# Exponentials over pairs of adjacent PSUM banks in an attention loop that also computes row maxima

## The chip, the cores and the metric

The kernel runs on one NeuronCore of a Trainium2 chip. A core has five engines that run their own instruction queues and meet through semaphores: TensorE (PE in the profile; its weight loads stand in a row of their own, PEld), VectorE (DVE), ScalarE (ACT), GpSimd (POOL) and SyncE (SP), which here issues DMAs. Matmul results land in PSUM, which has 8 banks; a bank holds 128 partitions of 512 fp32 values. The metric is the device time of one execution in microseconds.

## The reference, cut to what matters

Two blocks work on the same `x` of 2048 tokens by 640 channels, and a gate mixes them.

```python
g = sigmoid((x * gate_w).sum(-1, keepdims=True))
# attention: 32 heads of 20 channels, 2048 tokens
q, k, v = split(x @ wqkv)
scores = einsum("bhqd,bhkd->bhqk", q, k) * 20 ** -0.5
a = einsum("bhqk,bhkd->bhqd", softmax(scores), v) @ wo
# token-mixing MLP: over the token axis, 1728 hidden units
b = (gelu(layernorm(x)^T @ w1 + b1) @ w2 + b2)^T
out = g * a + (1 - g) * b
```

The change touches only the attention: scores, their exponentials and the sums with `v`.

## The kernel before, in words

Values are split into a high and a low part, so that fp32r matmuls (one pass) give nearly fp32 results: a product needs three of them. In the attention the three parts are stacked in the contraction instead, three times 20 rows a head. Two heads form a pair `p`; head `j=0` of a pair stands on partitions 0 to 63 and `j=1` on 64 to 127 of `ks` and `qs`, the two row halves of PE. Matmuls on different halves run side by side.

The softmax needs a maximum for each query. It is found one pair ahead: `s_next` runs one step of a stream, a matmul with queries on the partitions and 512 keys along the row (tile `s`, 60 rows of contraction, L178) and a VectorE reduction over it (L180). The stream takes the two halves in turn, `j=1` first. When the 64 tiles of half the queries are done, `s_max` and `s_store` gather the maxima, negate and split them, and send them through memory to two more rows of `qs`. So the score matmul in the loop itself (tile `st`, 62 rows of contraction, L700) gives score minus maximum, with keys on the partitions and queries along the row.

Before the loop come the projections and the MLP, into whose matmuls the first 736 of 2048 maximum tiles are mixed (`S_AHEAD`). The loop over the 16 pairs has 32 iterations for each, 512 in all: two halves of the queries (`qh`) by 16 blocks of 128 keys (`kt`). One iteration makes

- four score tiles of 128 keys by 512 queries, for `j` in two halves and `c` in two column blocks of 512 queries, each followed by an exponential on ScalarE (L703) that writes `p` to SBUF (`pt`, 12 buffers);
- `take` maximum tiles. The 1312 left (`LEFT`) are spread so that an iteration has two or three of them, and the last ones none;
- four products of `p` with `v` (tile `pv`, L637) on four column groups of PE, for the exponentials of the iteration before (`pend`, `pv_flush`); fp32 operands make two matmul instructions of each, eight in all. After 16 iterations `pv_evac` copies `pv` out on VectorE (L618), and POOL issues DMAs.

PE, ScalarE, VectorE, POOL and SP run in the order in which the program is written (`manual_schedule`). On PE an iteration is: score, maximum, score, maximum, score, maximum if `take` is 3, score, pv. `turn` chooses the halves so that a score tile and the maximum tile next to it lie on different halves. A PSUM tile is given out in turn from its tag's buffers; the matmul that reuses a buffer waits for the engine that read it. Tags are `st` (four banks), `s` (three banks) and `pv` (one): all eight banks. If `take` is 2, the third score tile takes a bank of `s` ("lent", L709). The same `st` tag serves the projections and the MLP ahead of the loop and the output product behind it.

Of the kernel before, what the change touches and what calls it, by code (L numbers as in the profile page):

```python
# [7 lines left out]
F32 = mybir.dt.float32  # L8
# [5 lines left out]
P = 128  # L14
S, D, H, DH, F = 2048, 640, 32, 20, 1728
# [13 lines left out]
def gated_mix(ctx, tc, xT, x, wqk, wv0, wv1, wo, w1, w1t, b1, w2, b2, out):  # L29
    nc = tc.nc  # L30
    EG = mybir.EngineType
    ctx.enter_context(tc.manual_schedule(engines={EG.PE}))
    PSUM = bass.MemoryType.PSUM
# [30 lines left out]
    cp = ctx.enter_context(tc.tile_pool(name="cp", bufs=1))  # L64
    base = ctx.enter_context(tc.tile_pool(name="base", bufs=1))
    psum = ctx.enter_context(tc.tile_pool(name="psum", bufs=1, space=PSUM))

    def st_tile(shape, name):
        return psum.tile(shape, F32, tag="st", bufs=4, name=name)

    def s_tile(shape, name):
        return psum.tile(shape, F32, tag="s", bufs=3, name=name)
# [44 lines left out]
    def base_stack(p, full, eng=nc.sync):  # L117
        ks = k8([P, S], F32R, f"ks{p}_{full}")
        qs = [q4([P, S // 2], F32R, f"qs{p}_{full}_{i}") for i in range(2)]
        load_stack(p, ks, qs, full, eng)  # L120
        return ks, qs

    def load_m(p, qs, half, put=nc.sync.dma_start):
        src = m_d[p, half].rearrange("(g i j t) r -> i j t g r", i=2, j=2, t=8)
        for j in range(2):
            for i in range(2):
                r = 64 * j + 3 * DH + i
                dst = qs[half].bitcast(F32)[r: r + 1, :].rearrange("o (t g r) -> o t g r", g=4, r=32)
                put(dst, src[i: i + 1, j])
# [3 lines left out]
    def load_v(p):  # L133
        v_tiles[p] = base.tile([P, NT, NPAIR], F32, tag="v", bufs=2, name=f"v{p}")
        c0 = NPAIR * (p % 8)
        nc.sync.dma_start(v_tiles[p], v_d[p // 8, :, :, c0: c0 + NPAIR].rearrange("t p c -> p t c"))
# [18 lines left out]
    def s_next():  # L155
        next(stream)()
        for e in list(s_close):
            e[0] -= 1
            if e[0] <= 0:
                s_close.remove(e)  # L160
                e[1]()

    def s_finish():
        next(stream, None)
        while s_close:
            s_close.pop(0)[1]()
# [46 lines left out]
    def qk_unit(m, w, q):  # L213
        wh, wl = w
        ps = st_tile([P, 512], f"qk{m}_{q}")
        mm3(ps, [(wh[:, c], wl[:, c], xh[c][q], xl[c][q]) for c in range(NC)])
        hi = p1.tile([P, 512], F32R, tag="evh", bufs=2, name=f"evh{m}_{q}")
        lo = p1.tile([P, 512], F32R, tag="evl", bufs=2, name=f"evl{m}_{q}")
        hi_lo(hi, lo, ps, hi_eng=nc.scalar)
        dst = q_d if m < NC else k_d  # L220
        rows = slice((m % NC) * P, (m % NC + 1) * P)
        cols = slice(q * 512, (q + 1) * 512)
        nc.sync.dma_start(dst[0, rows, cols], hi.bitcast(F32))
        nc.sync.dma_start(dst[1, rows, cols], lo.bitcast(F32))
# [12 lines left out]
    warm = p1.tile([P, 512], F32R, tag="evh", bufs=2, name="warm")  # L237
    nc.vector.memset(warm.bitcast(F32), 0.0)
    wps = st_tile([P, 512], "warm_ps")
    for i in range(10):  # L240
        nc.tensor.matmul(wps, warm[:, :P], warm, start=(i == 0), stop=(i == 9))
# [51 lines left out]
    for half in range(2):  # L293
        wvh, wvl = wvs[half]
        width = HALF + 2 if half == 0 else HALF
        for t in range(NT):
            n = NT * half + t
            if n == NT - 2:
                for i in range(4):
                    stats_load(i)  # L300
            if n == NT:
                nc.vector.tensor_scalar_mul(negm, gs[:, :, 1], -1.0 / D)
            if n in (2, 4, 6, 8, 10):
                split_wv(1, n // 2 - 1)
            if n == 2 * NT - 4:
                w[2] = load_w(2)
            ps = st_tile([P, width], f"v{half}_{t}")
            q, cols = t // 4, slice((t % 4) * P, (t % 4 + 1) * P)
            mm3(ps, [(xh[c][q][:, cols], xl[c][q][:, cols], wvh[c], wvl[c]) for c in range(NC)])
            vt = pvp.tile([P, 16, VW], F32, tag="vt", bufs=3, name=f"vt{half}_{t}")  # L310
            nc.gpsimd.memset(vt[:, :, DH], 1.0)
            nc.scalar.activation(vt[:, :, :DH], ps[:, :HALF].rearrange("p (h w) -> p h w", w=DH), AF.Copy)
            nc.sync.dma_start(v_d[half, t], vt.rearrange("p h w -> p (h w)"))
            if half == 0:
                nc.vector.tensor_copy(gs[:, t], ps[:, HALF:])
            else:
                stats_unit(t)
                stats_load(t + 4)
# [253 lines left out]
    lp = lps.enter_context(tc.tile_pool(name="lp", bufs=1, side="right"))  # L572

    def s_stack(p):
        ks = lp.tile([P, S], F32R, tag="sk", bufs=2, name=f"sk{p}")
        qs = [lp.tile([P, S // 2], F32R, tag="sq", bufs=4, name=f"sq{p}_{i}") for i in range(2)]
        load_stack(p, ks, qs, False)
        return ks, qs
# [52 lines left out]
    def pv_flush():  # L631
        while pend:
            p, qh, kt, pv, pts = pend.pop(0)
            for j in range(2):
                for c in range(2):
                    r = 32 * (2 * j + c)
                    nc.tensor.matmul(pv[r: r + 32, :], v_tiles[p][:, kt, 10 * j: 10 * j + 32], pts[j, c],  # L637
                                     start=(kt == 0), stop=(kt == NT - 1))
            if kt == NT - 1:
                pv_evac(p, qh, pv)  # L640
# [4 lines left out]
    def load_wo(c):  # L645
        raw = ap.tile([P, D], F32, tag="wor", bufs=1, name=f"wor{c}")
        nc.gpsimd.dma_start(raw, wo[c * P:(c + 1) * P, :])
        hi_lo(woh[c], wol[c], raw, hi_eng=nc.gpsimd, lo_eng=nc.gpsimd)
# [15 lines left out]
    def o_early(q, hi_eng=nc.scalar, lo_eng=nc.vector):  # L664
        o_hl[q] = o_part(q, slice(0, (NC - 1) * P), NC - 1, 256, "e", 2, hi_eng, lo_eng)
# [1 line left out]
    def o_late(q):  # L667
        return o_part(q, slice((NC - 1) * P, D), 1, 512, "l", 4, nc.scalar, nc.vector)[0]

    turn = given = 0  # L670
    LEFT = NP * 128 - S_AHEAD
    for p in range(NP):
        ks, qs = st_src[p]
        if 8 <= p < 8 + NC:
            load_wo(p - 8)
        for it in range(32):
            qh, kt = divmod(it, NT)
            if p + 1 < NP:
                if it == 6:
                    st_src[p + 1] = base_stack(p + 1, True)  # L680
                if it == 12:
                    load_v(p + 1)
                if it == 27:
                    load_m(p + 1, st_src[p + 1][1], 0)
            if it == 11 and p:
                load_m(p, qs, 1)
            if it == 14 and due_stack:
                n = due_stack.pop()
                if n < NP:
                    s_src[n] = s_stack(n)  # L690
            if p == NP - 1 and it in (20, 26):
                o_early(it // 26, nc.gpsimd, nc.gpsimd)
            if kt == 0:
                pv = psum.tile([P, 512], F32, tag="pv", bufs=1, name=f"pv{p}_{qh}")
            pts = {}

            def st_op(j, c, tile):
                r = slice(64 * j, 64 * j + 3 * DH + 2)
                ps = tile([P, 512], f"st{p}_{it}_{j}{c}")
                nc.tensor.matmul(ps, ks[r, kt * P:(kt + 1) * P], qs[qh][r, c * 512:(c + 1) * 512],  # L700
                                 start=True, stop=True)
                pt = lp.tile([P, 512], F32, tag="pt", bufs=12, name=f"p{p}_{it}_{j}{c}")
                nc.scalar.activation(pt, ps, AF.Exp, scale=SCALE)  # L703
                pts[j, c] = pt

            due = min((p * 32 + it + 1) * LEFT // (NP * 32 - 28) + 1, LEFT)
            take = min(due - given, 3)
            for n in range(4):
                st_op((n + turn) % 2, n // 2, s_tile if n == 2 and take < 3 else st_tile)  # L709
                if n < take:  # L710
                    s_next()
            given += take
            if take and given == LEFT:
                s_finish()
            turn = (turn + take) % 2
            pv_flush()
            if p * 32 + it in later:
                later.pop(p * 32 + it)()
            pend.append((p, qh, kt, pv, pts))
    pv_flush()  # L720
    ordered.close()
    lps.close()

    ep = ctx.enter_context(tc.tile_pool(name="ep", bufs=1, side="right"))
    tys = [ep.tile([P, 2, HALF], F32, name=f"oy{t}") for t in range(NT)]
# [13 lines left out]
    for t in range(NT):  # L739
# [5 lines left out]
        ps = [st_tile([P, HALF], f"a{t}_{i}") for i in range(2)]  # L745
        a_mms(t, ps, o_hl[t // 2], slice((t % 2) * P, (t % 2 + 1) * P), range(NC - 1))
    for t in range(NT):
        ps = [st_tile([P, HALF], f"b{t}_{i}") for i in range(2)]
# [49 lines left out]
```

## Time and profile before

| | us |
|---|---|
| median of 3 runs (1844.1 to 1847.46) | 1844.79 |
| the profiled execution: its span | 1844.8 |
| PE busy | 1829.7 |
| DVE busy | 1428.9 |
| ACT busy | 1361.6 |
| first and last exponential of the loop start | 699.5 and 1761.7 |

The span runs from the first to the last instruction and is the device time itself; nothing lies around it. In the rows of the profile, a group is a source line, engine, operation and tile, with its count, its busy time (overlaps counted once), the mean duration of one in ns, and the idle time of the engine just ahead of its instructions with what ended it. A busy share is not the share of time that work needs: neighbouring instructions of an engine overlap, and an engine whose instruction waits in its pipeline counts as busy. Timeline rows give the start, the length, the engine, the operation, how many were merged into the row, and in brackets the idle time ahead of it. The recorded ends of matmuls are modelled.

### The profile page before, as it was taken

How to read it: one execution, taken by the hardware profiler on the slowest of the kernel's cores; microseconds unless marked ns; L12 is line 12 of the kernel's file. 1: busy time of each engine (PE TensorE's matmuls, PEld its weight loads, DVE VectorE, ACT ScalarE, POOL GpSimd, SP SyncE). 2: the span in 40 equal slices, each digit the busy share in tenths (PEclk: the TensorE clock that was granted, in tenths of full speed). 3: DMA queues.
4: the chain of work that ended last, by engine and by line, in shares of the span. 5: the costliest groups of instructions: out<-in, count | busy, mean ns of one | idle time of the engine just before them, and what ended most of it. 6: DMA issues, size and time to landing. Idle time of an engine off the chain costs nothing. (4 is left out here: it accounts for less than half of the span.)

```text
span 1844.8 us, 39129 instructions
## 1 busy us (share of the span) xinstructions
PE 1829.7 (99%) x14978; PEld 1135.2 (62%) x14978; DVE 1428.9 (77%) x2341; ACT 1361.6 (74%) x2688; POOL 637.1 (35%) x900
## 2 busy tenths in 40 slices
PE   9999999999999999999999999999999999999998
PEld 7998799999999994333333333333333333333378
DVE  4202299999999998888888888888888888888137
ACT  4243244465444448999999999999999999999930
POOL 1013478888887770112112111121321211212210
PEclk9999999999999999999999999999999999999999
DMA  8456766566645645504032324213540423301463
GB/s 289 143 169 212 222 173 173 158 194 193 168 139 166 189 136 121 118 15 103 20 85 61 73 42 93 57 50 78 107 103 24 109 47 77 71 14 23 131 219 132
DMA packets 152831, 216.61 MB, mean 117 GB/s; under 512 B 65698, under 2 KB 92082, under 8 KB 148738
## 3 DMA queue, kind: packets, MB, share of 16 engines
q1 hardware_dynamic: 129172, 178.68, 35.4%
q0 software_dynamic: 14688, 20.78, 5.2%
q10 hardware_dynamic: 8784, 14.65, 2.4%
q8 instruction: 118, 1.93, 0.4%
q14 instruction: 69, 0.57, 0.1%
HBM read 165.43 MB, written 48.25 MB: 116 GB/s over the span
## 5 line engine op out<-in xcount | busy, mean ns | idle before, releaser
L180 DVE TENSOR_REDUCE mx<-s 128x1 f32<-128x512 f32 x2048 | 1293.7, 684 | 159.9 <-PE s L178 119.7
L703 ACT ACTIVATE p<-st 128x512 f32<-128x512 f32 x2048 | 1042.1, 615 | 20.9 <-PE s L178 2.2
L700 PEld LDWEIGHTS st<-qs_True,ks_True 62*128 62x128 f32 x2048 | 307.3, 185 | 485.1 <-ACT p L703 312.9
L700 PE MATMUL st<-qs_True,ks_True 62*128 62x512 f32 x2048 | 579.6, 425 | 0.2 <-ACT ty L477 0.2
L637 PE MATMUL pv<-p,v 128*32 128x512 f32 x4096 | 555.5, 605 | 0.2
L178 PE MATMUL s<-sk,sq 60*128 60x512 f32 x1280 | 423.1, 434 | 0.0
L41 POOL TENSOR_TENSOR wl<-wr,wh 128x512 fp32r<-128x512 f32 x228 | 273.6, 1216 | 59.8 <-ACT wh L38 30.9
L624 POOL DMA_DIRECT2D o_d<-oev x128 | 67.0, 524 | 494.3 <-DVE oev L618 491.6
L178 PE MATMUL s<-ks_False,qs_False 60*128 60x512 f32 x768 | 225.1, 397 | 0.4 <-DVE mx L180 0.3
L46 PE MATMUL y<-gh,wh 64*128 64x320 f32 x896 | 216.8, 308 | 0.0
L46 PE MATMUL y<-gl,wh 64*128 64x320 f32 x832 | 210.3, 306 | 0.0
L46 PE MATMUL y<-gh,wl 64*128 64x320 f32 x832 | 209.4, 305 | 0.0
L38 ACT ACTIVATE wh<-wr 128x512 fp32r<-128x512 f32 (+2 forms) x246 | 135.9, 594 | 90.2 <-PE s L178 29.0
L178 PEld LDWEIGHTS s<-sk,sq 60*128 60x128 f32 x1280 | 197.7, 185 | 1.2
L637 PEld LDWEIGHTS pv<-p,v 128*32 128x32 f32 x4096 | 84.9, 108 | 171.4 <-issue 156.4
L46 PE MATMUL u<-hl,wh 64*128 64x320 f32 x864 | 167.1, 306 | 0.0
L46 PE MATMUL u<-hh,wh 64*128 64x320 f32 x864 | 167.1, 306 | 0.0
L46 PE MATMUL u<-hh,wl 64*128 64x320 f32 x800 | 156.9, 306 | 0.4 <-POOL wl L41 0.4
L46 PEld LDWEIGHTS y<-gh,wh 64*128 64x128 f32 x896 | 155.3, 184 | 0.4
L46 PEld LDWEIGHTS y<-gh,wl 64*128 64x128 f32 x832 | 147.0, 184 | 0.3
L46 PEld LDWEIGHTS y<-gl,wh 64*128 64x128 f32 x832 | 146.9, 184 | 0.0
L178 PEld LDWEIGHTS s<-ks_False,qs_False 60*128 60x128 f32 x768 | 124.4, 184 | 1.1 <-DVE mx L180 1.1
(124 smaller groups left out, 1817.6 us busy)
## 6 DMA issues: line engine op xcount, KB each, us to landing
wr<-in_w_dram SPq DMA_DIRECT2D x196, 256.0 KB
ks_True<-k_d SPq DMA_DIRECT2D x96, 160.0 KB
qs_True<-q_d SPq DMA_DIRECT2D x192, 80.0 KB
sk<-k_d SPq DMA_DIRECT2D x60, 160.0 KB
sq<-q_d SPq DMA_DIRECT2D x120, 80.0 KB
v_d<-vt SPq DMA_DIRECT2D x32, 168.0 KB
v<-v_d SPq DMA_DIRECT2D x16, 336.0 KB
xr<-in_xT_dram SPq DMA_DIRECT2D x20, 256.0 KB
```

What stands on the lines that cost most here:

```text
L38: nc.scalar.activation(hi, src, AF.Copy)
L41: (lo_eng or nc.vector).tensor_sub(lo, src, hi.bitcast(F32))
L46: nc.tensor.matmul(ps[k], a[r], b[r], start=start, stop=stop)
L178: nc.tensor.matmul(ps, qs[half][r, t * P:(t + 1) * P], ks[r, kc * 512:(kc + 1) * 512], start=True, stop=True)
L180: nc.vector.tensor_reduce(mx[:, kc, j, t: t + 1], ps, axis=AX.X, op=OP.max)
L624: nc.gpsimd.dma_start(o_d[DH * h: DH * h + DH, cols], ev[r: r + DH, :])
L637: nc.tensor.matmul(pv[r: r + 32, :], v_tiles[p][:, kt, 10 * j: 10 * j + 32], pts[j, c], start=(kt == 0), stop=(kt == NT - 1))
L700: nc.tensor.matmul(ps, ks[r, kt * P:(kt + 1) * P], qs[qh][r, c * 512:(c + 1) * 512], start=True, stop=True)
L703: nc.scalar.activation(pt, ps, AF.Exp, scale=SCALE)
```

## The change

The two score matmuls of one column block, one for each head, write the two halves of one tile of two adjacent banks, and one exponential reads both banks, 1024 columns, and writes a `pt` tile of twice the width (6 buffers, the same bytes). An iteration has two such pairs, `c=0` and `c=1`, which take the two buffers of the tag `sp` in turn (four banks). The order on PE becomes: pair 0, two maximum tiles, pair 1, the third maximum tile if there is one, pv; with no maximum tiles pair 0, pair 1, pv. `first` chooses the half with which pair 1 starts. No score tile takes a bank of `s` any more. To make place for `sp`, the tag `st` moves to a pool that is closed ahead of the loop; another is opened behind it.

```diff
+    four = ExitStack()
+    banks = [four.enter_context(tc.tile_pool(name="four", bufs=1, space=PSUM))]
     def st_tile(shape, name):
-        return psum.tile(shape, F32, tag="st", bufs=4, name=name)
+        return banks[0].tile(shape, F32, tag="st", bufs=4, name=name)
...
-    turn = given = 0
+    four.close()
+    pairs = ExitStack()
+    pair_pool = pairs.enter_context(tc.tile_pool(name="pairs", bufs=1, space=PSUM))
+
+    given = 0
...
-            def st_op(j, c, tile):
-                r = slice(64 * j, 64 * j + 3 * DH + 2)
-                ps = tile([P, 512], f"st{p}_{it}_{j}{c}")
-                nc.tensor.matmul(ps, ks[r, kt * P:(kt + 1) * P], qs[qh][r, c * 512:(c + 1) * 512],
-                                 start=True, stop=True)
-                pt = lp.tile([P, 512], F32, tag="pt", bufs=12, name=f"p{p}_{it}_{j}{c}")
+            def st_pair(c, first):
+                ps = pair_pool.tile([P, 2, 512], F32, tag="sp", bufs=2, name=f"st{p}_{it}_{c}")
+                for j in (first, 1 - first):
+                    r = slice(64 * j, 64 * j + 3 * DH + 2)
+                    nc.tensor.matmul(ps[:, j], ks[r, kt * P:(kt + 1) * P], qs[qh][r, c * 512:(c + 1) * 512],
+                                     start=True, stop=True)
+                pt = lp.tile([P, 2, 512], F32, tag="pt", bufs=6, name=f"p{p}_{it}_{c}")
                 nc.scalar.activation(pt, ps, AF.Exp, scale=SCALE)
-                pts[j, c] = pt
+                for j in range(2):
+                    pts[j, c] = pt[:, j]
 
             due = min((p * 32 + it + 1) * LEFT // (NP * 32 - 28) + 1, LEFT)
             take = min(due - given, 3)
-            for n in range(4):
-                st_op((n + turn) % 2, n // 2, s_tile if n == 2 and take < 3 else st_tile)
-                if n < take:
-                    s_next()
+            st_pair(0, 0)
+            for n in range(take):
+                s_next()
+                if n == 1:
+                    st_pair(1, given % 2)
+            if take < 2:
+                st_pair(1, 0)
             given += take
...
-            turn = (turn + take) % 2
             pv_flush()
...
     ordered.close()
+    pairs.close()
     lps.close()
+    banks[0] = ctx.enter_context(tc.tile_pool(name="late", bufs=1, space=PSUM))
```

## The prediction

> **What bounds the kernel now.** The profiled execution spans 1844.8 us, the median of the runs is 1844.79, so the sum below is made against 1844.8 without a correction. I first read the busy times by stretch, to find the attention loop and what is full in it.
>
> ```profile
> 702.00:1710.00 1008.00, 1007.91 (x7122) 389.65 (x7122) 850.13 (x1387) 987.11 (x1938) 181.48 (x370) 1.00 0.31 68
> 1710.00:1762.00 52.00, 51.88 (x319) 15.41 (x314) 5.41 (x5) 52.00 (x108) 10.80 (x12) 1.00 0.36 116
> L703 ACT ACTIVATE p<-st 128x512 f32<-128x512 f32 x2048 | 1042.1, 615 | 20.9 <-PE s L178 2.2 <-PE st L700 0.3
> ```
>
> The columns are window, length, then PE, PEld, DVE, ACT and POOL busy. From 702 to 1762 us the loop runs. ACT is busy 987 of the first 1008 us, nearly all of it exponentials, and PE 1008. DVE has 16% to spare. Two engines look full, so the second view must tell which of them is late. It is the timeline of the weight loads, over three iterations with three, two and three maximum tiles:
>
> ```profile
> 848.10 0.18 PEld L700 LDWEIGHTS st<-qs_True,ks_True 62*128 62x128 f32 x1 [0.84 <-ACT p L703]
> 848.10 0.29 PEld L178 LDWEIGHTS s<-sk,sq 60*128 60x128 f32 x2
> ...
> 849.23 0.16 PEld L637 LDWEIGHTS pv<-p,v 128*32 128x32 f32 x8 [0.37 <-issue]
> 850.23 0.18 PEld L700 LDWEIGHTS st<-qs_True,ks_True 62*128 62x128 f32 x1 [0.84 <-ACT p L703]
> 850.23 0.29 PEld L178 LDWEIGHTS s<-sk,sq 60*128 60x128 f32 x2
> ...
> 851.14 0.16 PEld L637 LDWEIGHTS pv<-p,v 128*32 128x32 f32 x8 [0.35 <-issue]
> 852.13 0.18 PEld L700 LDWEIGHTS st<-qs_True,ks_True 62*128 62x128 f32 x1 [0.84 <-issue]
> ...
> 852.88 0.18 PEld L700 LDWEIGHTS st<-qs_True,ks_True 62*128 62x128 f32 x1 [0.20 <-ACT p L703]
> 853.30 0.16 PEld L637 LDWEIGHTS pv<-p,v 128*32 128x32 f32 x8 [0.24 <-issue]
> 854.30 0.18 PEld L700 LDWEIGHTS st<-qs_True,ks_True 62*128 62x128 f32 x1 [0.84 <-ACT p L703]
> ```
>
> The next iteration's first score load comes 1.00, 0.99 and 1.00 us after the first pv load, whether the view calls the gap a wait for ACT or "issue". A wait for ACT would vary; this is the length of the eight pv matmuls. So PE itself sets the pace. An iteration with three maximum tiles takes 2.13 us (848.10 to 850.23), with two 1.90 (850.23 to 852.13). The third is the exception: after a two-tile iteration a score load waits for an exponential at 852.88, and the stretch from start to pv is 1.17 instead of 1.13, a loss of 0.04. ACT's own idle time hides in the overlap of its rows:
>
> ```profile
> 848.10 0.49 PE L700 MATMUL st<-qs_True,ks_True 62*128 62x512 f32 x1
> 848.44 0.62 PE L700 MATMUL st<-qs_True,ks_True 62*128 62x512 f32 x2
> 848.91 0.40 PE L700 MATMUL st<-qs_True,ks_True 62*128 62x512 f32 x1
> 848.63 0.60 ACT L703 ACTIVATE p<-st 128x512 f32<-128x512 f32 x1
> 850.76 0.60 ACT L703 ACTIVATE p<-st 128x512 f32<-128x512 f32 x1
> ```
>
> The first score tile is done at 848.10+0.49 = 848.59 and its exponential starts at 848.63: ACT stood ready and waited for PE, in the next iteration too (first tile done about 850.72, exponential 850.76). PE's slots are 0.34 for the first concurrent pair (848.10 to 848.44), 0.24 for each of the next two ((848.91-848.44)/2), and 0.32 from the last slot to pv (848.91 to 849.23).
>
> **The change part by part.** *PE's own work.* Seven matmuls of an iteration still go two and two on opposite row halves, one alone, then pv; with two maximum tiles three pairs. Only the partners change (score with score, maximum with maximum). No matmul goes and no slot is saved: 0 us. The cover is that both partners lie on different halves, which two score tiles do already in the last pair of every two-tile iteration. If the new order made one slot a hundredth dearer or cheaper, 484 iterations would give 5 us either way.
>
> *ACT's work.* 2048 exponentials become 1024 of twice the columns. What one costs when nothing else limits shows at the loop's end, where no maximum tiles are left:
>
> ```profile
> 1710.40 0.66 ACT L703 ACTIVATE p<-st 128x512 f32<-128x512 f32 x1
> 1710.40 6.54 ACT L703 ACTIVATE p<-st 128x512 f32<-128x512 f32 x13
> 1716.61 0.83 ACT L703 ACTIVATE p<-st 128x512 f32<-128x512 f32 x1
> L38 ACT ACTIVATE ohl<-orl 128x512 fp32r<-128x512 f32 x4 | 2.5, 628 | 8.9 <-DVE orl L660 8.9
> L38 ACT ACTIVATE ohe<-ore 128x1024 fp32r<-128x1024 f32 x6 | 6.4, 1061 | 30.8 <-PE a L732 30.8
> L703 ACT ACTIVATE p<-st x2048: 588/603/855, 699.5 to 1761.7; 128x512 f32<-128x512 f32 x187
> L440 ACT ACTIVATE xg<-u 128x320 f32<-128x320 f32 x28 | 12.2, 434 | 53.7 <-PE u L46 53.7
> ```
>
> Thirteen starts in 6.21 us are 0.478 each; the ends, (1717.44-1711.06)/13, lie 0.491 apart. A copy of 1024 columns takes 1061-628 = 433 ns more than one of 512. So I estimate a wide exponential at 0.60+0.433 = 1.03 us alone, and its end 0.491+0.433 = 0.924 us after the end of one before it: ACT needs 1.85 instead of 1.96 an iteration. As PE paces, that saves nothing by itself. I take the slope of the copies because it spans the same step in width. The other rows for a slope, 320 to 512 columns out of PSUM, give (603-434)/192 x 512 = +0.451, hence 1.05 and 0.942, the high end; the starts' spacing, 0.478+0.433 = 0.911, is the low end.
>
> The Trainium skill, page "ScalarE: Activation LUTs", section "What ACT_TABLE_LOAD costs", gives 186 ns plus 0.833 ns a column, and neighbours that overlap by about 93 ns: 612 ns and a spacing of 520 at 512 columns. The trace has 603 and 478, so the measurement decides. By the page (an estimate) a wide one takes 1.04 and follows at 0.95, and the sum below would be some 10 us higher.
>
> *A second wait on every exponential.* In the changed kernel's built program nearly every wide exponential waits for two things, its matmuls and an exponential six back (long done); the first is taken by a semaphore instruction ahead of it. Before, 168 exponentials had that:
>
> ```profile
> L703 ACTq EVENT_SEMAPHORE  x168: 17/17/17, 698.8 to 1760.2; - x168
> 852.13 0.49 PE L700 MATMUL st<-qs_True,ks_True 62*128 62x512 f32 x1
> 852.21 0.62 ACT L703 ACTIVATE p<-st 128x512 f32<-128x512 f32 x1
> 852.21 1.11 ACT L703 ACTIVATE p<-st 128x512 f32<-128x512 f32 x2
> ```
>
> At 852.13 the matmul is done at 852.62; the second exponential of the last row ends at 853.32, so it started 0.60 earlier, at 852.72: 0.10 after its matmul, where the plain ones needed 0.04. Every first pair of an iteration pays these 0.06; the second pair's wait is satisfied while the first still runs, so I take 0 there (the high end is a rival).
>
> *Two pair buffers.* This is the term that decides. The second pair of an iteration refills the buffer that the second exponential of the iteration before leaves, and behind it on PE's queue stand the third maximum tile and pv. With an iteration starting at 0: matmuls done 0.49, exponential starts 0.59, ends 0.59+1.03 = 1.62, the second ends 0.924 later, 2.55. The row at 852.21 ends at 852.83 and releases the load at 852.88, 0.05 later: so the second pair's load goes at 2.60. A load that had to wait pays the first pair's slot of 0.34, then 0.32 for the last: pv at 3.26. Undisturbed, pv of the next iteration stands at its start plus 1.13: 3.03 after a two-tile iteration (1.90), 3.26 after a three-tile one (2.13). So after a three-tile iteration the wait is just covered, 0.00 lost, and after a two-tile one 0.23 is lost where 0.04 was. The exponential off the critical path now reaches it. The first pair never waits: its exponential ends at 1.62 and the load comes at 1.90 at the earliest. Three-tile iterations that lost 0.23 are long enough for the next second pair to be in time.
>
> How many: LEFT is 1312 maximum tiles in 484 iterations of two or three, so 344 of three, 140 of two (never two in a row), and 28 without. 140 x (0.23-0.04) = +26.6 us. After 204 three-tile iterations the margin is nil: 0 taken, up to 0.03 each (6 us) by the steeper slope.
>
> *The last 28 iterations.* There ACT paces now, with four times 0.491 = 1.96 us. By the same chain the second exponential ends at 2.55, the load goes at 2.60, pv 0.42 later (852.88 to 853.30), a next start 1.00 after that: 4.02 for two iterations, 2.01 each: +1.4 us.
>
> *No bank lent.* The third score tile of a two-tile iteration no longer takes a maximum bank:
>
> ```profile
> PEld st L700 <- DVE mx L180: 5.2, 20, 0.4
> PEld pv L637 <- DVE oev L618: 9.0, 23, 0.6
> L180 DVE TENSOR_REDUCE mx<-s 128x1 f32<-128x512 f32 x1175 | 743.4, 683 | 136.0 <-PE s L178 104.6 <-PE st L700 28.6
> ```
>
> Waits of score loads for DVE are 5.2 us; between 0 and -5.2 I take the middle, -2.6, since the maximum tiles keep their own waits. They come 0.24 later in the iteration (two after the first pair, one after the second). Three reductions take 3 x 743.4/1175 = 1.90 of 2.13 us, so DVE still catches up within the iteration; a pv copy or a closing of a half pushes it over, as it does now (the 9.0 us). I bound that by ±4 us, about half of this row, and take 0. Pool transitions ahead of and behind the loop: once each, 0. DMA queues, POOL and SP keep their order and are not moved past.
>
> Sum: 1844.8+26.6+1.4-2.6 = 1870.2.
>
> **The rivals.**
> *ACT paced it after all.* For it: 98% busy, and 311.7 us of waits put down to it:
>
> ```profile
> PEld st L700 <- ACT p L703: 311.7, 462, 1.7
> PEld st L700 <- issue: 138.3, 165, 0.8
> ```
>
> Then each wide exponential saves 2x0.491-0.924 = 0.058, 1024 of them 59 us: 1786. Against it: the 1.00 us that never varies, and ACT starting 0.04 after the first matmul. The point is whether score loads after pv really wait. The Trainium skill, page "Perfetto Trace Analysis", section "Identifying the Most-Contended Engine", says that matmul busy time is a poor measure and LDWEIGHTS busy a good one; by it PE, with 390 of 1008 us of loads, has headroom and this rival would win. The trace bears it out poorly here, since pv has short loads and long passes.
>
> *No wait comes up.* If the second wide exponential ends by 2.32, its load goes at 2.37, pv comes at 3.03 as undisturbed, and the second pair is in time everywhere. Then only the present waits go: 140 x 0.04 and 5.2 us, 1834; with a part of it, about 1840. Against it: from the start at 0.59 the two would need 1.73 us, 0.23 less than the rows give.
>
> *The semaphore instruction is not taken early.* If the second exponential also starts 0.06 later, the load goes at 2.66: 0.29 lost after a two-tile, 0.06 after a three-tile iteration: 140x0.25+204x0.06+28x0.08 = 49.5 us, less 2.6: 1892. For it: in the stretch shown the semaphore stands at an iteration's first exponential, where PE is late anyway, so the rows do not show the other case. Against it: ACT has nothing else to do there until the first exponential is through.
>
> **How the numbers follow.** A change under 0.2%, 3.7 us, can hardly be told from none. The forecast gets 0.63, its own range goes from 1861 (0.21 lost by the low end, all 5.2 gone, -4) to 1887 (0.26 lost and 0.03 after three-tile iterations by the high end, none of the 5.2 gone, +4). The later semaphore gets 0.16, no wait 0.12, ACT pacing 0.07, the rest goes to what I have not seen. Leaving out ACT pacing and the far half of "no wait", the range is 1840 to 1893. Faster: ACT pacing, two thirds of "no wait": 0.15. Same: the rest of it and the forecast's edge: 0.07. Slower: 0.78.
>
> **What would show it.** pv to the next score load stays 1.00 us. 1024 exponentials of 1.03 us or a little more, ACT some 930 us busy in the loop. Score loads waiting for ACT in the middle of an iteration, at the second pair, in iterations that follow a two-tile one, with start to pv at about 1.36 there and 1.13 elsewhere. The last 28 iterations at 2.0 us. I am wrong if start to pv after two-tile iterations stays near 1.17 (no wait), if it grows in all iterations (the semaphore, or a slower wide exponential), or if iterations fall below 1.90 (ACT paced).

## The result, and the profile after

The changed kernel takes 1871.75 us (median, 1870.8 to 1872.47), against 1844.44 for the kernel before on the same chip: 1.0143 times as long, 95% interval 1.0125 to 1.016. The forecast was 1870. The profiled execution spans 1869.7 us, 24.9 more than that of before. Its time is on record as 1871.45: here a time lies some 1.8 us above the span and is not the span itself. So below spans are compared with spans; the two medians differ by 27.3.

First the wide exponential, its group and its line in the trace of the changed kernel, and the waits of PE's loads in the loop (total, times, longest):

```profile
L710 ACT ACTIVATE p<-st x1024: 1016/1023/1045, 700.3 to 1786.8; 128x1024 f32<-128x1024 f32 x171
L710 ACTq EVENT_SEMAPHORE  x1019: 17/17/17, 700.2 to 1786.1; - x170
702.00:1735.00 1033.00, 1031.02 (x7129) 361.67 (x7128) 853.13 (x1389) 934.34 (x971) 181.29 (x370) 1.00 0.30 66
PEld st L707 <- ACT p L710: 526.5, 870, 0.9
PEld pv L639 <- DVE oev L620: 11.0, 27, 0.5
PEld s L180 <- DVE mx L182: 0.2, 1, 0.2
```

A wide exponential takes 1.02 us where two narrow ones were 0.60 each. ACT is busy 934 us of a longer stretch, where it was 987 of 1008: it has time to spare, and the kernel is slower. Of the 526.5 us that score loads wait for ACT, some 430 stand ahead of an iteration's first load, behind pv, where the gap is the length of pv's own work. The other 99 or so stand inside iterations; before, that was some 24. Where PE waits shows in the timeline of the weight loads, of a two-tile iteration (868.11) and the three-tile one that follows (870.00), beside the first one's two exponentials:

```profile
868.11 0.19 PEld L707 LDWEIGHTS st<-qs_True,ks_True 62*128 62x128 f32 x2 [0.84 <-ACT p L710]
868.22 0.19 PEld L180 LDWEIGHTS s<-sk,sq 60*128 60x128 f32 x2
...
869.00 0.16 PEld L639 LDWEIGHTS pv<-p,v 128*32 128x32 f32 x8 [0.25 <-issue]
870.00 0.19 PEld L707 LDWEIGHTS st<-qs_True,ks_True 62*128 62x128 f32 x2 [0.84 <-ACT p L710]
870.11 0.19 PEld L180 LDWEIGHTS s<-sk,sq 60*128 60x128 f32 x2
870.70 0.19 PEld L707 LDWEIGHTS st<-qs_True,ks_True 62*128 62x128 f32 x2 [0.40 <-ACT p L710]
870.81 0.19 PEld L180 LDWEIGHTS s<-sk,sq 60*128 60x128 f32 x1
871.35 0.16 PEld L639 LDWEIGHTS pv<-p,v 128*32 128x32 f32 x8 [0.36 <-issue]
872.35 0.18 PEld L707 LDWEIGHTS st<-qs_True,ks_True 62*128 62x128 f32 x2 [0.84 <-ACT p L710]
868.11 0.50 PE L707 MATMUL st<-qs_True,ks_True 62*128 62x512 f32 x2
868.71 1.02 ACT L710 ACTIVATE p<-st 128x1024 f32<-128x1024 f32 x1 [0.19 <-PE st L707]
869.63 1.02 ACT L710 ACTIVATE p<-st 128x1024 f32<-128x1024 f32 x1
```

The first pair's matmuls are done at 868.61 and the exponential starts at 868.71; the second starts 0.92 later and ends at 870.65. At 870.70 the next iteration's second pair is loaded, 2.59 after 868.11, and pv comes 1.35 after 870.00. In the kernel before such an iteration had 1.17. pv to the next score load is 1.00 as before.

All iterations of the two traces from the fourth on, told apart by their number of maximum tiles and by that of the iteration before, from the first score load to the first pv load (and the sum of their whole lengths):

```
                                    before              changed kernel
                           count  mean   sum us        mean   sum us
three tiles, after two      139   1.173   301.5        1.343   325.2
three tiles, after three    202   1.137   430.9        1.134   430.4
two tiles                   140   0.917   267.8        0.922   268.9
no tiles                     27           52.7                  54.4
```

The sums differ by +23.7, -0.5, +1.1 and +1.7. The fourth iteration starts at 706.7 before and at 706.1 now, -0.6 (the first score load comes 1.3 later, and the first three iterations make up for it); the stretch from the last iteration's start to the end is 0.5 shorter. That is the 24.9.

### The profile page after: what moved, and what is told of

It is laid out like the page before. It is cut to its first block, busy times and chain, and to the rows that moved or that the text cites. A ratio compares the mean times of both kernels' runs of the same rounds, so it can differ in the third digit from the quotient of the medians.

```text
span 1869.7 us, 38958 instructions
## 1 busy us (share of the span) xinstructions
PE 1848.0 (99%) x14978; PEld 1103.9 (59%) x14978; DVE 1430.3 (77%) x2341; ACT 1306.2 (70%) x1664; POOL 636.5 (34%) x900
## 5 line engine op out<-in xcount | busy, mean ns | idle before, releaser
L710 ACT ACTIVATE p<-st 128x1024 f32<-128x1024 f32 x1024 | 986.5, 1021 | 101.9 <-PE st L707 92.8
L639 PE MATMUL pv<-p,v 128*32 128x512 f32 x4096 | 546.7, 605 | 1.5 <-DVE oev L620 1.1
L707 PEld LDWEIGHTS st<-qs_True,ks_True 62*128 62x128 f32 x2048 | 192.2, 183 | 537.5 <-ACT p L710 527.4
L707 PE MATMUL st<-qs_True,ks_True 62*128 62x512 f32 x2048 | 478.0, 462 | 4.4 <-ACT p L710 2.9
L180 PE MATMUL s<-sk,sq 60*128 60x512 f32 x1280 | 318.7, 391 | 0.0
L639 PEld LDWEIGHTS pv<-p,v 128*32 128x32 f32 x4096 | 81.0, 108 | 169.5 <-issue 156.9
L46 PE MATMUL u<-hl,wh 64*128 64x320 f32 x864 | 170.9, 306 | 0.0
L46 PE MATMUL u<-hh,wl 64*128 64x320 f32 x800 | 160.7, 307 | 0.9 <-POOL wl L41 0.9
L180 PEld LDWEIGHTS s<-sk,sq 60*128 60x128 f32 x1280 | 152.9, 186 | 5.8
```

What stands on the lines that cost most here:

```text
L46: nc.tensor.matmul(ps[k], a[r], b[r], start=start, stop=stop)
L180: nc.tensor.matmul(ps, qs[half][r, t * P:(t + 1) * P], ks[r, kc * 512:(kc + 1) * 512], start=True, stop=True)
L707: nc.tensor.matmul(ps[:, j], ks[r, kt * P:(kt + 1) * P], qs[qh][r, c * 512:(c + 1) * 512], start=True, stop=True)
```

## The experiments

The kernel before ran again beside them: 1846.2 us beside "narrow", "last_after_two", "clustered" and "cols960", 1845.2 beside the other three. The ratios are to these. The iterations' means leave out the first three.

**The width undone, the order kept** ("narrow"): four single banks and 2048 exponentials, PE in the changed kernel's order.

```diff
-                ps = pair_pool.tile([P, 2, 512], F32, tag="sp", bufs=2, name=f"st{p}_{it}_{c}")
                 for j in (first, 1 - first):
                     r = slice(64 * j, 64 * j + 3 * DH + 2)
+                    ps = pair_pool.tile([P, 512], F32, tag="sp", bufs=4, name=f"st{p}_{it}_{j}{c}")
...
+                    pt = lp.tile([P, 512], F32, tag="pt", bufs=12, name=f"p{p}_{it}_{j}{c}")
+                    nc.scalar.activation(pt, ps, AF.Exp, scale=SCALE)
+                    pts[j, c] = pt
```

> The changed kernel's order on PE, but with four single banks and 2048 exponentials of 512 columns: the width alone undone. Theory (late release by ACT at the place where the second pair now stands): the two score tiles of the second pair are released one by one; the fourth exponential of the iteration before ends at 0.53+0.60+3x0.49 = 2.60 after its start, the last score load goes at 2.65, so start to pv is about 1.41 after a two-tile iteration and 1.18 after a three-tile one; 1885 to 1895 us, slower than the changed kernel. Rival (the wide exponential as such is what costs, by its late end or its semaphore): the time returns to 1845 to 1850 us, start to pv 1.17 after a two-tile iteration as in the kernel before.

Measured: 1881.72 us, 1.0194 [1.0179, 1.0209] of the kernel before, 10 us slower than the changed kernel. So the wide exponential is not what costs; the new order on PE is (the place of the second pair in it, as the next experiment shows), and the width wins a part back. The size was 3 us under the expectation's lower end. A two-tile iteration (871.24) and its follower in this kernel's weight loads:

```profile
871.24 0.19 PEld L707 LDWEIGHTS st<-qs_True,ks_True 62*128 62x128 f32 x2 [0.84 <-ACT p L710]
...
872.19 0.16 PEld L639 LDWEIGHTS pv<-p,v 128*32 128x32 f32 x8 [0.25 <-issue]
873.18 0.19 PEld L707 LDWEIGHTS st<-qs_True,ks_True 62*128 62x128 f32 x2 [0.84 <-ACT p L710]
873.29 0.19 PEld L180 LDWEIGHTS s<-sk,sq 60*128 60x128 f32 x2
873.53 0.19 PEld L707 LDWEIGHTS st<-qs_True,ks_True 62*128 62x128 f32 x1
873.88 0.18 PEld L707 LDWEIGHTS st<-qs_True,ks_True 62*128 62x128 f32 x1 [0.16 <-ACT p L710]
873.99 0.19 PEld L180 LDWEIGHTS s<-sk,sq 60*128 60x128 f32 x1
874.54 0.16 PEld L639 LDWEIGHTS pv<-p,v 128*32 128x32 f32 x8 [0.36 <-issue]
```

The third score tile goes at its undisturbed time, the fourth waits until 873.88, which is 2.64 after 871.24 (2.65 expected). Start to pv is 1.36 there and not 1.41, because two-tile iterations had grown too (0.95 from start to pv in the one shown; the median is 0.943, against 0.900 in the changed kernel), which gives the follower that much more time.

**The second pair one slot later** ("last_after_two"), only in three-tile iterations that follow a two-tile one:

```diff
             st_pair(0, 0)
+            at = 2 if take == 3 and (was == 2) else 1
             for n in range(take):
                 s_next()
-                if n == 1:
+                if n == at:
                     st_pair(1, given % 2)
...
+            was = take
```

> The changed kernel, but in a three-tile iteration that follows a two-tile one the second pair is issued behind the third maximum tile instead of ahead of it. Theory: the load of the second pair still goes at 2.60 after the start of the iteration before, but only 0.42 of work stands between it and pv, so pv comes at 3.02 where 3.03 is undisturbed: start to pv falls from 1.35 to about 1.13 in these 139 iterations, 139 x 0.21 = 29 us less, 1841 to 1845 us. Rival (the loss is the wide exponential's or the semaphore's own, spread over the loop): the time stays above 1860 us.

Measured: 1844.35 us, 0.9996 [0.9987, 1.0005]: the whole loss is gone. Only 139 of the 512 iterations were changed, and these add up to 296.6 us instead of 325.2, 28.6 less where 29 were expected. Its weight loads in such an iteration, behind a two-tile one that starts at 863.68 (868.11 and 870.00 above are its counterpart in the changed kernel):

```profile
863.68 0.19 PEld L707 LDWEIGHTS st<-qs_True,ks_True 62*128 62x128 f32 x2 [0.84 <-ACT p L710]
...
865.58 0.19 PEld L707 LDWEIGHTS st<-qs_True,ks_True 62*128 62x128 f32 x2 [0.84 <-ACT p L710]
865.69 0.42 PEld L180 LDWEIGHTS s<-sk,sq 60*128 60x128 f32 x3
866.27 0.19 PEld L707 LDWEIGHTS st<-qs_True,ks_True 62*128 62x128 f32 x2 [0.17 <-ACT p L710]
866.71 0.16 PEld L639 LDWEIGHTS pv<-p,v 128*32 128x32 f32 x8 [0.25 <-issue]
```

The pair's load still waits for ACT and goes at the same 2.59 (866.27 after 863.68), but the third maximum tile has gone ahead of it, and pv comes 1.13 after the start. The wait is there and costs nothing.

**The same for all three-tile iterations** ("last_always"), with `at = 2 if take == 3 else 1`.

> As last_after_two, but in every three-tile iteration the second pair stands behind the third maximum tile. Theory (three maximum banks are just enough with the third tile in the last slot): a third maximum tile asked for one slot earlier meets a bank whose reduction ends 2.69 after the start of the iteration before, its load goes at 2.74 instead of by 2.59, 0.15 lost in every second iteration that follows a three-tile one; waits of maximum loads for DVE appear, 1855 to 1866 us. Rival (DVE has room, the order matters only for the second pair): as last_after_two, 1841 to 1845 us.

Measured: 1862.19 us, 1.0092 [1.0076, 1.0108], as the theory had it. The 202 iterations of three tiles after three rise from a mean of 1.141 (last_after_two) to 1.216, 15 us in all, and a wait that the changed kernel had for 0.2 us appears:

```profile
PEld s L180 <- DVE mx L182: 50.3, 191, 0.4
```

So the third maximum tile cannot be moved ahead at will: three maximum banks carry it only in the last slot, unless the iteration before asked for two.

**Two-tile iterations side by side** ("clustered"): the same numbers, sorted in blocks of 44.

```diff
+    for n in range(0, 484, 44):
+        takes[n: n + 44] = sorted(takes[n: n + 44], reverse=True)
...
-            take = min(due - given, 3)
+            take = takes[p * 32 + it]
```

> The changed kernel with the same number of two- and three-tile iterations, put together: in every block of 44 iterations first all three-tile ones, then all two-tile ones. Theory (a chain over two iterations): in a run of two-tile iterations every second one pays 0.22 at its second pair, because one that has paid is long enough for the next; about 70 losses instead of 139, 1856 to 1859 us. Rival (each two-tile iteration causes one wait of fixed length, or a cost of the new order): 1870 to 1873 us.

Measured: 1862.35 us, 1.0089 [1.0074, 1.0104], 9 us faster than the changed kernel and 3 above the expectation. A run of two-tile iterations in its weight loads:

```profile
963.39 0.19 PEld L714 LDWEIGHTS st<-qs_True,ks_True 62*128 62x128 f32 x2 [0.84 <-ACT p L717]
...
964.08 0.18 PEld L714 LDWEIGHTS st<-qs_True,ks_True 62*128 62x128 f32 x2 [0.39 <-ACT p L717]
964.52 0.16 PEld L639 LDWEIGHTS pv<-p,v 128*32 128x32 f32 x8 [0.25 <-issue]
965.51 0.19 PEld L714 LDWEIGHTS st<-qs_True,ks_True 62*128 62x128 f32 x2 [0.84 <-ACT p L717]
966.41 0.16 PEld L639 LDWEIGHTS pv<-p,v 128*32 128x32 f32 x8 [0.24 <-issue]
967.41 0.19 PEld L714 LDWEIGHTS st<-qs_True,ks_True 62*128 62x128 f32 x2 [0.84 <-ACT p L717]
968.54 0.16 PEld L639 LDWEIGHTS pv<-p,v 128*32 128x32 f32 x8 [0.25 <-issue]
```

Start to pv alternates, 1.13, 0.90, 1.13: every second one pays, which a fixed cost of a two-tile iteration would not do. The 129 two-tile iterations that follow one take 2.02 us in the mean, where half of 2.59+0.43+1.00 is 2.01 and 1.90 is undisturbed. Where the 3 us above the expectation come from was not taken apart.

**Shorter exponentials** ("cols960", "cols768"): each covers 2x480, or 2x384, of 2x512 columns; `p` has constant 1.0 in the columns left out, so that a part of the exponentials isn't computed. The edit of "cols960"; "cols768" has `EC = 384`:

```diff
+    EC = 480
+    fixed = [lp.tile([P, 2, 512], F32, name=f"ptf{i}") for i in range(6)]
+    for i in range(6):
+        nc.gpsimd.memset(fixed[i][:, :, EC:], 1.0)
...
-                nc.scalar.activation(pt, ps, AF.Exp, scale=SCALE)
+                pt = fixed[(2 * (p * 32 + it) + c) % 6]
+                nc.scalar.activation(pt[:, :, :EC], ps[:, :, :EC], AF.Exp, scale=SCALE)
```

> The changed kernel, but each exponential covers 2x480 of its 2x512 columns (the rest of p is a constant, so 1/16 of the exponentials is left out). 64 columns fewer are 64 x 0.846 = 54 ns less for each. Theory: the second pair's load goes 2 x 54 ns = 0.11 earlier, start to pv after a two-tile iteration falls from 1.35 to 1.24, the rest stays at 1.13: 139 x 0.11 and 28 x 0.05, 1855 us. Rival (ACT paces): 1024 x 54 ns = 55 us less, 1816 us. Rival (a fixed cost of order, pools or semaphore): 1870 us.

> The changed kernel with exponentials over 2x384 of 2x512 columns (the rest of p is a constant, so a quarter of the exponentials is left out). Theory (PE is the floor under the wait): each exponential is 256 x 0.846 = 217 ns shorter, twice the 0.22 that the wait is long, so start to pv after a two-tile iteration stops at 1.13; the last 28 iterations fall to about 1.75: 1834 to 1840 us. Rival (the loss goes on falling in proportion, ACT paces): four times the 14.6 us that 1/16 of the columns gave, 1813 us.

Measured: 1857.13 us, 1.0065 [1.0048, 1.0082], and 1835.32, 0.9947 [0.9932, 0.9962]. The exponentials' groups in the two traces, and the means from the first score load to pv (1024 columns are the changed kernel):

```profile
L714 ACT ACTIVATE ptf<-st 128x960 f32<-128x960 f32 x1022 | 936.1, 968 | 133.8 <-PE st L711 116.5 <-PE s L180 8.9
L714 ACT ACTIVATE ptf<-st 128x768 f32<-128x768 f32 x1022 | 772.7, 808 | 276.8 <-PE st L711 262.4 <-PE s L180 13.1
```

```
columns   one, ns   three tiles after two   three after three   median us
1024        1021          1.343                  1.134           1871.75
 960         968          1.249                  1.131           1857.13
 768         808          1.127                  1.132           1835.32
```

53 ns less in each of two exponentials take 0.094 off the one kind of iteration and next to nothing off the other; four times that reaches the floor of 1.13 and stays there, though ACT then idles 277 us in the loop. PE is the floor; ACT's release is what stands above it. The last is 0.5% below the kernel before, but with a quarter of the exponentials missing it is no version to keep. Nor is all of that the second pair's wait: against the kernel before, the iterations after a two-tile one are 6.4 us shorter (295.1 for 301.5), and another 4.3 come from the last 28 (48.4 for 52.7), where ACT had set the pace.

**Order and width crossed** ("narrow_last"): "narrow" with the order of "last_after_two".

> last_after_two with 2048 exponentials of 512 columns in four single banks: with it and the runs so far, order and width stand crossed. Theory (PE paces, width is worth only what the release of the last score tile gains): start to pv after a two-tile iteration about 1.17, against 1.13 with wide exponentials, 1845 to 1852 us. Rival (the wide exponential's shorter ACT time is worth something by itself): over 1860 us. Rival (the wide exponential's semaphore costs): under 1842 us.

Measured: 1857.72 us, 1.0067 [1.0045, 1.009]: outside all three expectations.

```
median us                       512 columns    1024 columns
changed kernel's order            1881.72        1871.75
second pair later after two       1857.72        1844.35
```

The two-tile followers came as expected (1.156, 1.17 expected). The miss is mostly in the iterations of three after three: a mean of 1.173, against 1.141 with wide exponentials. I had put 0.05 lost there into the expectation of "narrow" and forgot it here: 202 x 0.032 is 6.5 us, and two-tile iterations and the last 28 add 3 us. So in this order the shorter ACT time is worth 13 us after all. The chain above accounts for most of it: the last score load goes at 2.66 (the median after three-tile iterations) instead of 2.60, and 2.60 is just ahead of the point where it begins to cost. No run tells this apart from any other effect of the width.

## Why the prediction was right, point by point

*What bounds the kernel: right.* From the fourth iteration to the last one with maximum tiles, pv to the next score load stayed between 0.99 and 1.08 us in every kernel, and with a quarter of ACT's work gone the iterations stopped at the same 0.90 and 1.13. The rival in which ACT paces fell with "cols768": the time did not go on falling in proportion, to 1813 us. The Trainium skill, page "Perfetto Trace Analysis", section "Identifying the Most-Contended Engine", judges TensorE's headroom by MFU (the share of its peak that its matmuls reach) and by the busy time of LDWEIGHTS. By the second, with 362 of 1033 us of loads in the changed kernel's loop, PE would have much headroom; the trace does not agree, for those 0.90 and 1.13 stayed.

*PE's own work at 0: right.* Undisturbed, start to pv is 0.900 with two maximum tiles in both kernels, and 1.132 before and 1.130 now with three (medians).

*Cost of a wide exponential: right, a little high.* 1.02 us for 1.03, and 0.92 to the next as estimated; the slope between 768 and 1024 columns is (1021-808)/256 = 0.83 ns a column, not the copies' 0.846.

*The second wait: right.* 0.10 from matmul to exponential at an iteration's first pair (868.61 to 868.71, and so in nearly all iterations), nothing at the second: the starts lie 0.92 apart. The rival of a late semaphore, which would have put the load at 2.66, falls with the measured 2.59.

*Two pair buffers: right, and it is nearly the whole loss.* Load at 2.59 (2.60), start to pv 1.35 (1.36), three-tile iterations after three untouched. The term was +26.6 and measured 23.7. It is 139 iterations and not 140, since the last two-tile one has no three-tile one behind it, and 12 of them lose nothing (1.11 to 1.14): there the two-tile iteration ahead had itself waited (1.11 to 1.19), which made it long enough to cover the wait. The mean is 1.343, the median 1.35; before, the mean was 1.173 as put. "last_after_two" takes the loss away at its place, "clustered" shows the chain over two iterations, the shorter exponentials its dependence on the release. That it would take the new order to make this wait, and not the width, the prediction did not say; "narrow" shows it.

*The last 28 iterations: right.* 2.01 us each as put; +1.7 for +1.4.

*No bank lent: wrong, by some 3 us.* The score loads' 5.2 us of waits for DVE are gone from the table of waits. All 20 of them stood in two-tile iterations, but these did not gain: 268.9 us now for 267.8. Twelve of them, at the start of a block of 16 iterations, now take 1.11 to 1.19 from start to pv; in eight PE waits for DVE's copy of `pv`, in four the second pair waits for ACT. With the -0.5 of the three-tile iterations after three that is +0.6 for -2.6. The half was taken without a reason that the trace gave.

*Pool transitions at 0: right on balance.* The first score load does wait for the banks of the closed pool:

```profile
699.42 0.47 PEld L707 LDWEIGHTS st<-qs_True,ks_True 62*128 62x128 f32 x2 [1.39 <-ACT x L454]
```

L454 is ScalarE's last reading of the MLP's PSUM tiles, and all eight kernels with the new pools show the same 1.39. But the next iterations are quicker, and the fourth starts 0.6 earlier than before. In the other kernels it starts anywhere from 705.1 to 708.7, so a difference of this size at the loop's start means little.

*No wait comes up: fell.* The wait came. That "cols768" ends at 1835 us, near this rival's 1834, does not speak for it: work is left out there, and 4.3 us of its gain come from the last 28 iterations, which the rival had left as they were.

*The sum: closer than its terms.* It gave +25.4 and the spans differ by 24.9. The deciding term carried it, but that the two agree within 1 us is luck: -2.9 in the deciding term, +0.3 in the last iterations, +3.2 at the banks, -0.6 at the loop's start and -0.5 behind it happen to cancel.

## What to carry to other kernels

When the engine that sets the pace has work in its queue behind a wait, what counts is not how much faster the other engine does its work but when it gives back the buffer, measured against the slot in which that buffer is next asked for: 2.59 us after an iteration's start was harmless behind a 2.13 us iteration and cost 0.2 behind a 1.90 us one. Here two small buffers became one wide one, which halved the count of releases, and the new order moved the asking forward; work out such a chain over two rounds, for the shortest round and not the mean. Before giving such a change up, look for work that may go ahead of the waiting instruction: here a change of three lines brought back 27 us, though the same order in every three-tile iteration ran into the next buffer limit.

## What the runs showed that I had not expected

The order alone, with narrow exponentials, is slower (1881.72 us) than the order with wide ones: the part of the change that looked like the gain was a gain, and the harmless-looking regrouping on PE was the loss. And the kernel with both put right (1844.35 us) only equals the one before, 0.9996 [0.9987, 1.0005]. Leaving out a quarter of the exponentials brought no more than 1835.32 us, with the iterations at PE's own slots; what another order of PE's work could give was not tried. No version that does the whole computation came out faster than the kernel before.
